# A linear-attention and two-MLP kernel: PSUM shared out anew in the attention, its rounds in nine stretches of like tiling, projections apart from their Vector steps

## The chip, the cores and the metric

The kernel runs on one core of a Trainium2 chip. The metric is the device time of one execution in microseconds (us). Before the change three timed runs gave a median of 804.03 us (803.39 to 804.15).

## What is computed

```python
def phi(x):                                   # x: 4 batches, 8 heads, 576 tokens, 64
    proj = einsum('bhsd,df->bhsf', x, w_phi)  # 128 features
    proj = proj - max(abs(proj), axis=-1)
    return concatenate([exp(proj), exp(-proj)], axis=-1)
q_p, k_p = phi(q), phi(k)
kv  = einsum('bhsf,bhsd->bhfd', k_p, v)
z   = sum(k_p, axis=2)
num = einsum('bhsf,bhfd->bhsd', q_p, kv)
den = einsum('bhsf,bhf->bhs', q_p, z)[..., None] + 1e-06
x = (num / den), heads side by side           # 4 x 576 x 512
h = relu(x @ w_in)                            # 512 -> 1024
conv_out = depthwise convolution of h over 3 tokens with conv_w
x = (h * sigmoid(conv_out)) @ w_out           # 1024 -> 512
u = x + mixing of the tokens through rank 32 (U, V)
out = u + relu(u @ w_ch1) @ w_ch2             # 512 -> 2048 -> 512
```

The activations and q, k, v, w_phi are float32. The other weights are stored as 64-bit numbers and are decoded on the chip into a high and a low part.

## The kernel before

The attention comes first, in eight rounds of four heads each (two pairs of heads; a batch has two rounds). A pair fills the 128 partitions, 64 for each head. The 1152 columns of a round, two pairs of 576 tokens, are cut into three groups of three 128-blocks for either pair. After the attention come the gated layer (`hp` at L610, `x2p` at L662), the mixing of tokens, and the second MLP (`hps` at L859, `po` at L881).

One round i does this, all of it in float32:

- TensorE (PE) projects each of three k groups and three q groups with w (`ppk`, `ppq`, six products of 64x128 each, L289), into a pair of PSUM banks. Vector (DVE) centres the pair into d: a reduction to the largest absolute value (L292) and a subtraction (L294). In the code both are one function, `centred`.
- ScalarE (ACT) makes the k features `ek` from dk (two exponentials, L303 and L304). For q PE first turns the centred group (`tq`, six transposes, L319, into a pair of banks), and ACT makes `et` out of it (two exponentials, L328).
- PE sums `kvp` out of ek and v for either pair (L339) and the sums of ek, `zp` (L353). ACT evicts both (`kt`, `zt`), PE turns them (`pk` L374, `pz` L388), ACT evicts again (`kv` L381, `z` L395).
- PE makes the numerators (`np`, four single banks a round, L407) and the denominators (`dp`, two banks, L432), ACT evicts them as `num` (L418) and `den` (L440).
- The division: four transfers on the queue of SyncE (SP) lay den out over 128 partitions (`dent`, L443), Vector takes the reciprocal (`rec`, in `divide`), one transfer writes it out (`recd`, L451), four read it back spread over 64 partitions each (`rb`, L458), and GpSimd (POOL) multiplies num by rb into `xf` (L462; in the last round Vector does). ScalarE and Vector split xf of the first batch into a high part `xh` (L227) and a low part `xl` (L233) for the gated layer.

Beside this, fourteen pieces of the gated layer's weights (`win`, `wout`, 512 KB each) are decoded, two in a round. A piece is a generator (`split_steps`) that `go_on` moves on by one step: its load on SP (L166) into a raw buffer, of which the pool `stage` has two under that tag; two steps on Vector (L77, L80); a square and the low half on ScalarE (L86, L88); two steps on Vector (L96, L99) and a product on POOL (L100); a cast on ScalarE (L174) and a subtraction and an addition on POOL (L175, L176). L176 is the last to read the raw buffer. `cw_steps` does the same for the small convolution weights, at the very start. The q, k and v of a round are loaded by SP a round ahead, each into one of two buffers.

PSUM has eight banks. In the attention two pools share them:

```python
ps_s = att_ctx.enter_context(tc.tile_pool(name="ps_s", bufs=4, space=PSUM))
ps_p = front_ctx.enter_context(tc.tile_pool(name="ps_p", bufs=2, space=PSUM, side="right"))
```

A tile of `ps_s` is one bank (kvp, zp, np, dp, ...), a tile of `ps_p` a pair (pp, tq). A step that takes a new tile waits until the readers of the tile that had its place are done.

The order is written by hand. `front` is a list of steps, each with a lag: in turn i of the loop a step with lag -1 works for round i-1. On PE, Vector and ScalarE the instructions stand in the order in which this list issues them (`manual_schedule`). On the queues of SP and of POOL the framework's scheduler puts them in order, and there they run one after the other: an instruction that waits holds up all that stand behind it.

Of the kernel before, what the change touches and what calls it, by code (L numbers as in the profile page):

```python
# [18 lines left out]
P = 128  # L19
# [5 lines left out]
def kernel(  # L25
# [103 lines left out]
    def cw_steps():  # L129
        n = 3 * NJ  # L130
        raw = stage.tile([P, 512, 2], I32, tag="raw", name="cw_raw")[:, 0:n, :]
        x = stage.tile([P, 512], I32, tag="x", name="cw_x")[:, 0:n]
        nc.scalar.dma_start(out=raw.rearrange("p n t -> p (n t)"), in_=conv_w.bitcast(I32))
        yield
        widen_head(raw, x)
        yield
        square_and_low(raw)
        yield
        xf, low = widen_rest(raw, x, nc.gpsimd)
        yield  # L140
        nc.vector.tensor_add(cw, xf, low)
        yield
# [126 lines left out]

    def loads_kv(i):  # L270
        for g in range(G):
            load_part("k", k, i, g)
        load_part("q", q, i, 0)
        t = fpool.tile([P, 10, 2, D], F32, tag="v", name=f"v{i}")
        nc.sync.dma_start(out=t.rearrange("p t h d -> p (t h d)"), in_=v[i])
        raw["v", i] = t

    def loads_q(i):
        for g in range(1, G):
            load_part("q", q, i, g)  # L280

    def centred(nm, i, g):
        x = raw.pop((nm, i, g))
        pp = ps_p.tile([P, 2, 512], F32, tag="p", name=f"pp{nm}{i}_{g}")
        for t in range(G):
            c = slice(t * P, (t + 1) * P)
            for s in range(2):
                r = slice(s * D, (s + 1) * D)
                nc.tensor.matmul(pp[:, s, c], lhsT=x[r, c], rhs=w2[r, :], start=True, stop=True)  # L289
        pv = pp[:, :, 0:GC].rearrange("p s (t f) -> p s t f", f=P)  # L290
        m = fpool.tile([P, 2, G, 1], F32, tag="m", name=f"m{nm}{i}_{g}", bufs=4)
        nc.vector.tensor_reduce(out=m[:, :, :, 0], in_=pv, op=ALU.max, axis=AX.X, apply_absolute_value=True)  # L292
        d = fpool.tile([P, 2, G, P], F32, tag="d", name=f"d{nm}{i}_{g}", bufs=3)
        nc.vector.tensor_tensor(out=d, in0=pv, in1=m.to_broadcast([P, 2, G, P]), op=ALU.subtract)  # L294
        return d

    def k_centred(i, g):
        state[i]["dk"].append(centred("k", i, g))

    def k_features(i, g):  # L300
        d = state[i]["dk"][g].rearrange("p s t f -> p (s t) f")
# [3 lines left out]
        state[i]["es"].append(e)  # L305

    def k_tile(i, s, t):
        return state[i]["es"][t // G][:, s * G + t % G, :, :].rearrange("p a f -> p (a f)")

    def q_centred(i, g):  # L310
        state[i]["ds"].append(centred("q", i, g))

    def turn_q(i, g):
        st = state[i]
        d = st["ds"][g]
        ps = ps_p.tile([P, 2, 512], F32, tag="p", name=f"tq{i}_{g}")
# [5 lines left out]
    def q_features(i, g):  # L322
        st = state[i]
        if g == 0:
            st["et"] = apool.tile([P, 2, 2, PT], F32, tag="et", name=f"et{i}", bufs=1)
# [6 lines left out]
    def kv(i, u):  # L332
        st = state[i]
        if u == 0:
            st["kvp"] = ps_s.tile([P, 512], F32, tag="s", name=f"kvp{i}")
# [61 lines left out]
    def numerators(i, u):  # L397
        st = state[i]
        st["np"] = []
        for c in range(2):  # L400
            ps = ps_s.tile([P, 512], F32, tag="s", name=f"np{i}_{u}{c}")
            st["np"].append(ps)
            cs = slice(u * S + c * HC, u * S + (c + 1) * HC)
# [7 lines left out]
    def evict_numerators(i, u):  # L411
# [3 lines left out]
        else:  # L415
            num = apool.tile([P, S], F32, tag="num", name=f"num{i}_{u}", bufs=2)
        for c, ps in enumerate(st.pop("np")):
            nc.scalar.copy(num[:, c * HC : (c + 1) * HC], ps[:, 0:HC])  # L418
# [26 lines left out]
    def divide(i):  # L445
        st = state.pop(i)
        b, g = divmod(i, H // 4)
# [20 lines left out]
    def new(i):  # L468
        state[i] = {"es": [], "ds": [], "dk": [], "tq": {}}

# [9 lines left out]
    def go_on(n):  # L480
        if n in under_way:
            next(under_way[n])

    def step(f, *args):
        return lambda i: f(i, *args)

    def first(i):
        go_on(2 * i - 1)

    def second(i):  # L490
        go_on(2 * i)

# [4 lines left out]
    def first_rests(i):  # L497
        if 4 <= i < 4 + NK:
            split_rest(0, i - 4)

    front = [
        (new, 0),
        (step(k_centred, 0), 0),
        (turn_kv, -1),
        (turned_kv, -1),
        (step(turn_q, 2), -1),
        (step(q_features, 2), -1),
        (turn_sums, -1),
        (turned_sums, -1),
        (first, 0),  # L510
        (first_rests, 0),
        (step(k_features, 0), 0),
        (step(numerators, 0), -1),
        (step(evict_numerators, 0), -1),
        (first, 0),
        (step(k_centred, 1), 0),
        (step(numerators, 1), -1),
        (step(k_features, 1), 0),
        (step(evict_numerators, 1), -1),
        (step(k_centred, 2), 0),  # L520
        (lambda i: begin_piece(2 * i), 0),
        (first, 0),
        (denominators, -1),
        (step(k_features, 2), 0),
        (evict_denominators, -1),
        (first, 0),
        (first_heads, 0),
        (step(q_centred, 0), 0),
        (loads_kv, 1),
        (step(kv, 0), 0),  # L530
        (step(q_centred, 1), 0),
        (loads_q, 1),
        (step(turn_q, 0), 0),
        (step(q_features, 0), 0),
        (divide, -1),
        (second, 0),
        (step(kv, 1), 0),
        (evict_kv, 0),
        (second, 0),
        (step(q_centred, 2), 0),  # L540
        (second, 0),
        (step(turn_q, 1), 0),
        (step(q_features, 1), 0),
        (second, 0),
        (lambda i: begin_piece(2 * i + 1), 0),
        (sums, 0),
        (evict_sums, 0),
    ]

    loads_kv(0)  # L550
    loads_q(0)

    under_way[-1] = cw_steps()
    go_on(-1)
    att_order, rounds_order = ExitStack(), ExitStack()
    att_order.enter_context(tc.manual_schedule(engines={mybir.EngineType.PE}))
    rounds_order.enter_context(tc.manual_schedule(engines={mybir.EngineType.DVE, mybir.EngineType.Activation}))
    for i in range(NU):
        for step, lag in front:
            if 0 <= i + lag < NU:  # L560
                step(i + lag)
    i = NU - 1
    turn_kv(i)
    turned_kv(i)
    turn_q(i, 2)
    q_features(i, 2)
    turn_sums(i)
    turned_sums(i)
# [3 lines left out]
    for u in range(2):  # L572
        numerators(i, u)
        evict_numerators(i, u)
    denominators(i)
    evict_denominators(i)
    rounds_order.close()
# [411 lines left out]
```

## Time and profile before

| | |
|---|---|
| median of three runs | 804.03 us (803.39 to 804.15) |
| the profiled execution | 804.7 us, of which its span, first to last instruction, is 802.9 us |
| mean granted clock of TensorE | 0.997 of full speed |
| TensorE (PE) busy | 792.5 us, 99% of the span |
| Vector (DVE) busy | 521.0 us, 65% |
| ScalarE (ACT) busy | 351.8 us, 44% |
| GpSimd (POOL) busy | 105.5 us, 13% |
| DMA, mean over the span | 72 GB/s |

A row of the timeline gives the start of a group of like instructions in us from the span's start, the time to the end of the last of them, the engine, the line, the operation with its tiles (output <- inputs, numbers left out) and shapes, and xN, the records in the group. Where an engine was idle ahead of a group, a bracket gives that time and what ended it. A matmul's end is modelled, so a PE row can end a little after the next one starts; starts are the better rulers. SPq is SP's queue of DMA issues: its duration is that of the issuing and says nothing of when the data lands.

### The profile page before, as it was taken

What the parts mean: (1) busy time and instruction counts of PE and PEld (TensorE: products, weight loads), DVE (VectorE), ACT (ScalarE), POOL (GpSimd) and SP (SyncE); (2) the same over time, 40 slices, a digit from 0 to 9 for tenths busy, and PEclk for the clock granted to TensorE, in tenths of its full rate; (3) what the DMA queues carried; (4) which work ended last, traced back from release to release, by engine and by line L of the source; (5) the groups of instructions that cost most, each with busy time, mean ns of one, the idle gap of its engine ahead of it and who ended that gap; (6) DMA issues with size and microseconds to landing.
All of it is one profiled execution on the core that took longest, in us unless ns stands there. A gap on an engine that the chain in (4) does not pass through costs nothing.

```text
span 802.9 us, 12634 instructions
## 1 busy us (share of the span) xinstructions
PE 792.5 (99%) x5082; PEld 640.0 (80%) x5082; DVE 521.0 (65%) x825; ACT 351.8 (44%) x625; POOL 105.5 (13%) x112
## 2 busy tenths in 40 slices
PE   8999999999999999999999999999999999999997
PEld 6666666669998888988778788888888888888886
DVE  5777888856989978975368734883496285332322
ACT  4777877776677754654314312341242132111010
POOL 0354445430201220210000000000000000000000
PEclk9999999999999999999999999999999999999999
DMA  7355455412221120112221101220120020000212
GB/s 234 106 176 175 144 156 173 133 32 84 52 69 53 31 96 1 55 52 79 91 78 55 53 0 53 78 81 1 53 77 29 0 80 27 0 1 1 91 66 79
DMA packets 34650, 58.12 MB, mean 72 GB/s; under 512 B 7008, under 2 KB 21472, under 8 KB 34592
## 3 DMA queue, kind: packets, MB, share of 16 engines
q1 hardware_dynamic: 34304, 57.23, 22.4%
q8 instruction: 40, 0.66, 0.3%
q14 instruction: 18, 0.15, 0.1%
q10 hardware_dynamic: 288, 0.09, 0.0%
HBM read 48.77 MB, written 8.46 MB: 71 GB/s over the span
## 4 chain that ended last, share of the span: by engine, by line
PE 82%; DVE 10%; DMA 4%; ACT 2%; issue 1%; SPq 0%; POOL 0%; DVEq 0%; ACTq 0%; POOLq 0%
PE hps L859 23%; PE po L881 23%; PE hp L610 7%; PE x2p L662 7%; PE kvp L339 4%; PE np L407 3%; PE ppk L289 3%; PE ppq L289 2%; PE zp L353 2%; DVE cv L622 2%; PE tq L319 2%; PE dp L432 2%; PE x2m L680 1%; DVE g L630 1%; PE utp L818 1%
## 5 line engine op out<-in xcount | busy, mean ns | idle before, releaser
L865 ACT ACTIVATE hh<-hps 128x512 fp32r<-128x512 f32 (+1 forms) x80 | 44.3, 553 | 223.5 <-PE hps L859 218.9
L866 DVE SCALAR_TENSOR_TENSOR hl<-hps,hh 128x512 fp32r<-128x512 f32 (+1 forms) x80 | 50.8, 635 | 101.6 <-ACT hh L865 101.6
L610 PE MATMUL hp<-xh,win 128*128 128x288 f32 x512 | 105.0, 296 | 0.0
L662 PE MATMUL x2p<-wout,g 128*128 128x512 f32 x384 | 96.1, 392 | 0.5 <-ACT g L629 0.5
L859 PE MATMUL hps<-uh,c1h 128*128 128x512 f32 (+1 forms) x240 | 88.9, 371 | 0.7 <-ACT x L642 0.7
L859 PE MATMUL hps<-ul,c1h 128*128 128x512 f32 (+1 forms) x240 | 88.4, 368 | 0.0
L859 PE MATMUL hps<-uh,c1l 128*128 128x512 f32 (+1 forms) x240 | 88.3, 368 | 0.0
L610 PEld LDWEIGHTS hp<-xh,win 128*128 128x128 f32 x512 | 83.7, 188 | 4.5 <-issue 2.1
L886 DVE TENSOR_TENSOR u<-u,po 128x512 f32<-128x512 f32 x90 | 58.5, 682 | 41.0 <-PE po L881 41.0
L881 PE MATMUL po<-c2h,hh 128*128 128x512 f32 x216 | 84.3, 390 | 0.0
L881 PE MATMUL po<-c2l,hh 128*128 128x512 f32 x216 | 84.2, 390 | 0.0
L881 PE MATMUL po<-c2h,hl 128*128 128x512 f32 x216 | 82.0, 389 | 0.0
L662 PEld LDWEIGHTS x2p<-wout,g 128*128 128x128 f32 x384 | 69.7, 188 | 14.0 <-ACT g L629 0.9
L610 PE MATMUL hp<-xl,win 128*128 128x288 f32 x256 | 75.6, 295 | 0.0
L622 DVE SCALAR_TENSOR_TENSOR cv<-h,cw,cv 128x576 f32<-128x576 f32 x64 | 51.5, 812 | 6.6 <-ACT cv L620 6.2
L859 PEld LDWEIGHTS hps<-uh,c1h 128*128 128x128 f32 x240 | 45.2, 188 | 9.5 <-ACT x L642 1.1
L859 PEld LDWEIGHTS hps<-uh,c1l 128*128 128x128 f32 x240 | 45.2, 188 | 7.8
L859 PEld LDWEIGHTS hps<-ul,c1h 128*128 128x128 f32 x240 | 45.2, 188 | 7.9
L610 PEld LDWEIGHTS hp<-xl,win 128*128 128x128 f32 x256 | 48.2, 188 | 1.7 <-issue 0.8
L655 POOL CAST ghold<-g 128x128 fp32r<-128x128 f32 x32 | 27.2, 854 | 168.9 <-DVE g L630 161.8
L881 PEld LDWEIGHTS po<-c2h,hh 128*128 128x128 f32 x216 | 40.6, 188 | 8.6 <-ACT hh L865 0.8
L881 PEld LDWEIGHTS po<-c2h,hl 128*128 128x128 f32 x216 | 40.6, 188 | 8.6
(490 smaller groups left out, 1447.3 us busy)
## 6 DMA issues: line engine op xcount, KB each, us to landing
v<-in_v_dram SPq DMA_DIRECT2D x8, 640.0 KB, 4.8
kr<-in_k_dram SPq DMA_DIRECT2D x24, 192.0 KB, 3.7
qr<-in_q_dram SPq DMA_DIRECT2D x24, 192.0 KB, 3.7
rb<-recd SPq DMA_DIRECT2D x32, 144.0 KB, 3.5
out_dram<-u SPq DMA_DIRECT2D x18, 256.0 KB, 2.1
u<-x2d SPq DMA_DIRECT2D x14, 256.0 KB, 3.9
x2d<-x SPq DMA_DIRECT2D x10, 256.0 KB, 2.2
c_0r<-in_moe_w_ch_dram SPq DMA_DIRECT2D x2, 512.0 KB, 4.3
```

The lines of the kernel that those rows point to most:

```text
L289: nc.tensor.matmul(pp[:, s, c], lhsT=x[r, c], rhs=w2[r, :], start=True, stop=True)
L339: nc.tensor.matmul(o[s * D : (s + 1) * D, :], lhsT=raw["v", i][:, 5 * u + n, s, :], rhs=k_tile(i, s, 4 * u + n), start=(n == 0), stop=(n = ...
L407: nc.tensor.matmul(ps[r, 0:HC], lhsT=st["kv"][:, u, a, r], rhs=st["et"][:, s, a, cs], start=(a == 0), stop=(a == 1))
L610: nc.tensor.matmul(ps[:, 0:HC], lhsT=win[kk][:, wi, j * P : (j + 1) * P], rhs=xs[b][kk][xi][:, cs], start=(i == 0), stop=(i == 3 * NK - 1),)
L622: nc.vector.scalar_tensor_tensor(out=cv, in0=h[:, t : t + S], scalar=cw[:, t * NJ + j : t * NJ + j + 1], in1=cv, op0=ALU.mult, op1=ALU.add,)
L655: nc.gpsimd.tensor_copy(ghold[:, :, j, off : off + LEFT], g.bitcast(F32)[:, :, rest : rest + LEFT])
L662: nc.tensor.matmul(x2p[t], lhsT=g[:, gi, ts_], rhs=w[wi], start=(j == 0 and i == 0), stop=(j == NJ - 1 and i == 2),)
L859: nc.tensor.matmul(ps[:, 0:w], lhsT=ch[j, 0][wi][:, kc], rhs=x[:, kk, :], start=(n == 0), stop=(n == 3 * NK - 1))
L865: nc.scalar.activation(hh, ps[:, 0:w], AF.Relu)
L866: nc.vector.scalar_tensor_tensor(out=hl, in0=ps[:, 0:w], scalar=0.0, in1=hh.bitcast(F32), op0=ALU.max, op1=ALU.subtract)
L881: nc.tensor.matmul(po[i][t], lhsT=x[:, cs], rhs=w, start=(j == js[0] and n == 0), stop=(j == js[-1] and n == 2))
L886: nc.vector.tensor_add(u, u, p)
```

## The change

- **PSUM.** `ps_s` has two single banks and `ps_p` three pairs, for four and two.
- **Projection apart from centring.** `centred` becomes `project` (PE) and `centre` (Vector), two steps that the list may put apart. A projection's buffer is loaded for the next round right behind it (`project_and_load`), v two rounds ahead (`load_v`).
- **The list `front`** is written anew: ppk_0; pk and pz and tq_2; ppk_1 and ppk_2; the four np; ppq_1, ppq_0, ppq_2; the two dp; kvp of both pairs; tq_0 and tq_1; zp. Vector centres the q groups in the order 1, 0, 2, the last of them at the end of the turn.
- **The pieces** begin at other places, two in a turn as before; the two loads stand before the denominators' eviction. The convolution weights move from the start into round 7, and their load from ScalarE's queue to SP's.

Cut to its core:

```diff
-        nc.scalar.dma_start(out=raw.rearrange("p n t -> p (n t)"), in_=conv_w.bitcast(I32))
+        nc.sync.dma_start(out=raw.rearrange("p n t -> p (n t)"), in_=conv_w.bitcast(I32))
...
-    ps_s = att_ctx.enter_context(tc.tile_pool(name="ps_s", bufs=4, space=PSUM))
-    ps_p = front_ctx.enter_context(tc.tile_pool(name="ps_p", bufs=2, space=PSUM, side="right"))
+    ps_s = att_ctx.enter_context(tc.tile_pool(name="ps_s", bufs=2, space=PSUM))
+    ps_p = front_ctx.enter_context(tc.tile_pool(name="ps_p", bufs=3, space=PSUM, side="right"))
...
-    def centred(nm, i, g):
+    def project(i, nm, g):
...
                 nc.tensor.matmul(pp[:, s, c], lhsT=x[r, c], rhs=w2[r, :], start=True, stop=True)
+        state[i]["pp", nm, g] = pp
+
+    def centre(i, nm, g):
+        pp = state[i].pop(("pp", nm, g))
...
+    def project_and_load(i, nm, g):
+        project(i, nm, g)
+        if i + 1 < NU:
+            load_part(nm, {"k": k, "q": q}[nm], i + 1, g)
...
     def first(i):
-        go_on(2 * i - 1)
+        go_on(2 * i - 2)
     def second(i):
-        go_on(2 * i)
+        go_on(2 * i + 1)
+    def begin_first(i):
+        begin_piece(2 * i - 2)
+    def begin_second(i):
+        begin_piece(2 * i + 1)
...
+    front = [
+        (first, 0), (first_heads, -1),
+        (step(turn_q, 0), -1), (step(turn_q, 1), -1), (evict_kv, -1),
+        (step(q_features, 0), -1), (sums, -1), (step(q_features, 1), -1), (evict_sums, -1),
+        (step(project_and_load, "k", 0), 0),
+        (second, -1), (turn_kv, -1), (turn_sums, -1), (turned_kv, -1), (first, 0),
+        (step(centre, "k", 0), 0),
+        (begin_first, 1), (turned_sums, -1), (second, -1),
+        (step(turn_q, 2), -1), (step(q_features, 2), -1),
+        (step(project_and_load, "k", 1), 0), (step(project_and_load, "k", 2), 0),
+        (back[0], -1),
+        (step(centre, "k", 1), 0), (step(centre, "k", 2), 0),
+        (back[1], -1), (back[2], -1), (second, -1),
+        (step(project_and_load, "q", 1), 0), (step(project_and_load, "q", 0), 0),
+        (first_rests, -1), (step(k_features, 0), 0),
+        (step(project_and_load, "q", 2), 0),
+        (back[3], -1), (begin_second, 0),
+        (step(centre, "q", 1), 0),
+        (back[4], -1), (step(k_features, 1), 0),
+        (step(centre, "q", 0), 0),
+        (back[5], -1), (step(k_features, 2), 0),
+        (first, 1), (divide, -1), (second, 0), (first, 1),
+        (step(kv, 0), 0), (step(kv, 1), 0), (load_v, 2),
+        (step(centre, "q", 2), 0),
+    ]
```

Here `back[0]` to `back[5]` are the numerators of pair 0, their eviction, those of pair 1, theirs, the denominators and their eviction. In the last turn the steps of lag -1 are issued once more for the last round, `back` after the pools of the front are closed, as before.

How this moves the instructions is shown at three places. Names of tiles carry a group or bank number and a running number, and line numbers are those of the program that the row is of. The first place is PE in the middle of a round, with the numerators and denominators of the round before; the program before:

```order
L289 MATMUL ppk_1_384<-w_117,kr_1_220 128x128 x6
L407 MATMUL np_10_395<-et_261,kv_348 64x288 x4
L407 MATMUL np_11_400<-et_261,kv_348 64x288 x4
L289 MATMUL ppk_2_411<-w_117,kr_2_222 128x128 x6
L432 MATMUL dp_0_429<-et_261,z_362 32x288 x8
L432 MATMUL dp_1_438<-et_261,z_362 32x288 x8
L289 MATMUL ppq_0_461<-w_117,qr_0_224 128x128 x6
L339 MATMUL kvp_482<-ek_0_366,v_226 64x256 x6
L339 MATMUL kvp_482<-ek_1_405,v_226 64x256 x4
L289 MATMUL ppq_1_493<-w_117,qr_1_250 128x128 x6
L319 MATMUL tq_0_508<-ident,dq_0_470 128x128 x6
```

and the same stretch of the changed one:

```order
L277 MATMUL ppk_1_368<-w_117,kr_1_176 128x128 x6
L277 MATMUL ppk_2_377<-w_117,kr_2_185 128x128 x6
L393 MATMUL np_00_386<-et_294,kv_341 64x288 x4
L393 MATMUL np_01_391<-et_294,kv_341 64x288 x4
L393 MATMUL np_10_407<-et_294,kv_341 64x288 x4
L393 MATMUL np_11_412<-et_294,kv_341 64x288 x4
L277 MATMUL ppq_1_420<-w_117,qr_1_202 128x128 x6
L277 MATMUL ppq_0_429<-w_117,qr_0_211 128x128 x6
L277 MATMUL ppq_2_441<-w_117,qr_2_223 128x128 x6
L418 MATMUL dp_0_460<-et_294,z_354 32x288 x8
L418 MATMUL dp_1_469<-et_294,z_354 32x288 x8
```

Products of one kind that stood apart now stand side by side, and the four np come one behind the other into two single banks, where they had four.

The second place is SP and POOL in the turn in which the weight pieces win30 and win31 are loaded. SP's queue before:

```order
L267 DMA kr_0_1010<-in_k_dram 128x384
L166 DMA win30r<-in_moe_w_in_dram 128x1024
L267 DMA kr_1_1012<-in_k_dram 128x384
L267 DMA kr_2_1014<-in_k_dram 128x384
L267 DMA qr_0_1016<-in_q_dram 128x384
L443 DMA dent_989<-den_986 32x1x18 x4
L267 DMA qr_1_1042<-in_q_dram 128x384
L166 DMA win31r<-in_moe_w_in_dram 128x1024
L451 DMA recd_96<-rec_1056 128x18
L275 DMA v_1290<-in_v_dram 128x1280
L458 DMA rb_0_1060<-recd_96 64x576 x2
```

and in the changed program:

```order
L267 DMA kr_2_920<-in_k_dram 128x384
L166 DMA win30r<-in_moe_w_in_dram 128x1024
L267 DMA qr_1_963<-in_q_dram 128x384
L166 DMA win31r<-in_moe_w_in_dram 128x1024
L267 DMA qr_0_972<-in_q_dram 128x384
L267 DMA qr_2_984<-in_q_dram 128x384
L429 DMA dent_1024<-den_1021 32x1x18 x4
L437 DMA recd_96<-rec_1034 128x18
L481 DMA v_1073<-in_v_dram 128x1280
L444 DMA rb_0_1038<-recd_96 64x576 x2
L444 DMA rb_1_1043<-recd_96 64x576 x2
```

Both loads of a turn stand ahead of dent, where one stood behind it and ahead of recd. POOL's queue for the two pieces of that turn's raw buffers before:

```order
L462 TENSOR_TENSOR xf_0_793<-num_0_647,rb_0_790 128x576
L100 TENSOR_TENSOR win20r<-win20r 128x512
L175 TENSOR_TENSOR win20x<-win20x,win_690 128x512
L462 TENSOR_TENSOR xf_1_798<-num_1_676,rb_1_795 128x576
L176 TENSOR_TENSOR win_690<-win20x,win20r 128x512
L100 TENSOR_TENSOR win21r<-win21r 128x512
L175 TENSOR_TENSOR win21x<-win21x,win_690 128x512
L176 TENSOR_TENSOR win_690<-win21x,win21r 128x512
```

and in the changed program:

```order
L100 TENSOR_TENSOR win20r<-win20r 128x512
L448 TENSOR_TENSOR xf_0_773<-num_0_672,rb_0_770 128x576
L448 TENSOR_TENSOR xf_1_778<-num_1_718,rb_1_775 128x576
L175 TENSOR_TENSOR win20x<-win20x,win_618 128x512
L100 TENSOR_TENSOR win21r<-win21r 128x512
L176 TENSOR_TENSOR win_618<-win20x,win20r 128x512
L175 TENSOR_TENSOR win21x<-win21x,win_618 128x512
L176 TENSOR_TENSOR win_618<-win21x,win21r 128x512
```

The first piece's product moved ahead of the two xf, and both xf stand ahead of both pieces' L176.

The third place is ScalarE at the end of the attention, in the changed program; before, the casts and copies stand in the same order, with the copy z between the second and the third cast:

```order
L314 ACTIVATE et_2157<-tq_2_2202 128x2x384 x2
L227 CAST xh_0_2466<-xf_0_1041 128x576
L227 CAST xh_1_2470<-xf_1_1046 128x576
L227 CAST xh_2_2474<-xf_0_1311 128x576
L227 CAST xh_3_2478<-xf_1_1316 128x576
L404 COPY num_0_2232<-np_00_2222 128x288
L404 COPY num_0_2232<-np_01_2227 128x288
L404 COPY num_1_2245<-np_10_2235 128x288
```

The four casts `xh` of the second batch still stand ahead of the copy that frees the bank of np_00, and np_10 now takes that bank.

## Rows read from the trace of the kernel before

**Rows 1.** The page, busy time of each engine.

```profile
PE 792.5 (99%) x5082; PEld 640.0 (80%) x5082; DVE 521.0 (65%) x825; ACT 351.8 (44%) x625; POOL 105.5 (13%) x112
```

**Rows 2.** Timeline of PE, two attention rounds (start, us, engine line op).

```profile
22.59 0.94 PE L289 MATMUL ppk<-w,kr 64*128 64x128 f32 x12
...
45.41 0.82 PE L319 MATMUL tq<-ident,dq 128*128 128x128 f32 x6
46.06 0.38 PE L388 MATMUL pz<-ident,zt 128*128 128x128 f32 x2
46.37 2.16 PE L407 MATMUL np<-et,kv 128*64 128x288 f32 x16
48.47 0.94 PE L289 MATMUL ppk<-w,kr 64*128 64x128 f32 x12
...
58.42 0.87 PE L319 MATMUL tq<-ident,dq 128*128 128x128 f32 x6
59.22 2.38 PE L339 MATMUL kvp<-ek,v 128*64 128x256 f32 x20
...
65.50 0.94 PE L289 MATMUL ppk<-w,kr 64*128 64x128 f32 x12
```

**Rows 3.** Windows, 10 to 12 us: PE, PEld, DVE, ACT, POOL, clock, DMA, GB/s.

```profile
10.00:12.00 2.00, 2.00 (x16) 1.58 (x17) 1.83 (x4) 1.72 (x3) 0.00 (x0) 0.51 0.99 382
```

**Rows 4.** Timeline of DVE, the start, and the end of a weight step.

```profile
5.63 0.96 DVE L292 TENSOR_REDUCE mk<-ppk 128x6 f32<-128x768 f32 x1 [5.63 <-PE ppk L289]
...
7.50 0.17 DVE L77 TENSOR_SCALAR cw_x<-cw_raw 128x24 int32<-128x24 int32 x1
...
64.45 0.68 DVE L96 SCALAR_TENSOR_TENSOR win20x<-win20r,win20x 128x512 f32<-128x512 f32 x1
65.17 0.43 DVE L99 TENSOR_SCALAR win20r<-win20x 128x512 int32<-128x512 int32 x1
```

**Rows 5.** Timeline of SP's queue, three rounds of the division.

```profile
35.19 3.74 SPq L443 DMA_DIRECT2D dent<-den  x4
...
97.62 0.33 SPq L166 DMA_DIRECT2D wout00r<-in_moe_w_out_dram  x1
...
99.55 2.44 SPq L443 DMA_DIRECT2D dent<-den  x4
...
104.19 0.33 SPq L451 DMA_DIRECT2D recd<-rec  x1
...
107.39 1.13 SPq L458 DMA_DIRECT2D rb<-recd  x2
...
168.65 0.34 SPq L451 DMA_DIRECT2D recd<-rec  x1
170.12 2.40 SPq L458 DMA_DIRECT2D rb<-recd  x4
```

**Rows 6.** Timeline of POOL, one round (the releaser of idle time in brackets).

```profile
111.94 1.73 POOL L462 TENSOR_TENSOR xf<-num,rb 128x576 f32<-128x576 f32 x1 [9.17 <-DMA rb<-recd]
...
115.15 1.27 POOL L175 TENSOR_TENSOR wout00x<-wout00x,wout 128x512 f32<-128x512 f32 x1
116.38 1.43 POOL L462 TENSOR_TENSOR xf<-num,rb 128x576 f32<-128x576 f32 x1
117.76 1.31 POOL L176 TENSOR_TENSOR wout<-wout00x,wout00r 128x512 fp32r<-128x512 f32 x1
120.21 1.04 POOL L100 TENSOR_TENSOR wout01r<-wout01r 128x512 f32<-128x512 f32 x1 [1.15 <-issue]
```

**Rows 7.** Timeline of PE and ACT at the end of the attention.

```profile
174.22 4.10 PE L407 MATMUL np<-et,kv 128*64 128x288 f32 x32
...
180.61 0.53 PE L610 MATMUL hp<-xh,win 128*128 128x288 f32 x2
...
175.51 1.25 ACT L227 CAST xh<-xf 128x576 fp32r<-128x576 f32 x2
...
178.06 1.32 ACT L418 COPY num<-np 128x288 f32<-128x288 f32 x4
```

More of the change, by code (lines that the diff above doesn't have):

```diff
@@ L268, in load_part @@
         raw[nm, i, g] = t
[L270 to L280, printed above, removed]
-    def centred(nm, i, g):
+    def project(i, nm, g):
         x = raw.pop((nm, i, g))
@@ L323, in q_features @@
         st = state[i]
-        if g == 0:
+        if "et" not in st:
             st["et"] = apool.tile([P, 2, 2, PT], F32, tag="et", name=f"et{i}", bufs=1)
@@ L333, in kv @@
         st = state[i]
-        if u == 0:
+        if "kvp" not in st:
             st["kvp"] = ps_s.tile([P, 512], F32, tag="s", name=f"kvp{i}")
@@ L416, in evict_numerators @@
             num = apool.tile([P, S], F32, tag="num", name=f"num{i}_{u}", bufs=2)
-        for c, ps in enumerate(st.pop("np")):
+        for c, ps in enumerate(st.pop(("np", u))):
             nc.scalar.copy(num[:, c * HC : (c + 1) * HC], ps[:, 0:HC])
@@ L466 @@
     pieces += [lambda j=j: wout_piece(j) for j in range(NJ - 2)]
-    def new(i):
-        state[i] = {"es": [], "ds": [], "dk": [], "tq": {}}
+    pieces += [None, cw_steps]
+    for i in range(NU):
+        state[i] = {"es": {}, "tq": {}}
     under_way = {}
@@ L499, in first_rests @@
             split_rest(0, i - 4)
-    front = [
-        (new, 0),
-        (step(k_centred, 0), 0),
+    back = [
+        step(numerators, 0),
+        step(evict_numerators, 0),
+        step(numerators, 1),
+        step(evict_numerators, 1),
+        denominators,
+        evict_denominators,
+    ]
+    front = [
+        (first, 0),
+        (first_heads, -1),
+        (step(turn_q, 0), -1),
+        (step(turn_q, 1), -1),
+        (evict_kv, -1),
+        (step(q_features, 0), -1),
+        (sums, -1),
+        (step(q_features, 1), -1),
+        (evict_sums, -1),
+        (step(project_and_load, "k", 0), 0),
+        (second, -1),
@@ L504 @@
         (turn_kv, -1),
+        (turn_sums, -1),
         (turned_kv, -1),
+        (first, 0),
+        (step(centre, "k", 0), 0),
+        (begin_first, 1),
+        (turned_sums, -1),
+        (second, -1),
         (step(turn_q, 2), -1),
         (step(q_features, 2), -1),
[L508 to L511, printed above, removed]
-        (step(k_features, 0), 0),
-        (step(numerators, 0), -1),
-        (step(evict_numerators, 0), -1),
-        (first, 0),
@@ L516 @@
-        (step(k_centred, 1), 0),
-        (step(numerators, 1), -1),
-        (step(k_features, 1), 0),
[L519 to L523, printed above, removed]
-        (step(k_features, 2), 0),
[L525 to L531, printed above, removed]
@@ L532 @@
-        (loads_q, 1),
-        (step(turn_q, 0), 0),
-        (step(q_features, 0), 0),
+        (step(project_and_load, "k", 1), 0),
+        (step(project_and_load, "k", 2), 0),
+        (back[0], -1),
+        (step(centre, "k", 1), 0),
+        (step(centre, "k", 2), 0),
+        (back[1], -1),
+        (back[2], -1),
+        (second, -1),
+        (step(project_and_load, "q", 1), 0),
+        (step(project_and_load, "q", 0), 0),
+        (first_rests, -1),
+        (step(k_features, 0), 0),
@@ L535 @@
+        (step(project_and_load, "q", 2), 0),
+        (back[3], -1),
+        (begin_second, 0),
+        (step(centre, "q", 1), 0),
+        (back[4], -1),
+        (step(k_features, 1), 0),
+        (step(centre, "q", 0), 0),
+        (back[5], -1),
+        (step(k_features, 2), 0),
+        (first, 1),
         (divide, -1),
         (second, 0),
+        (first, 1),
+        (step(kv, 0), 0),
         (step(kv, 1), 0),
-        (evict_kv, 0),
-        (second, 0),
-        (step(q_centred, 2), 0),
@@ L541 @@
[L541 to L547, printed above, removed]
-    ]
[L550 to L554, printed above, removed]
+        (load_v, 2),
+        (step(centre, "q", 2), 0),
+    ]
+    for g in (0, 1, 2):
+        load_part("k", k, 0, g)
+    load_part("q", q, 0, 1)
+    load_v(0)
+    for g in (0, 2):
+        load_part("q", q, 0, g)
@@ L555 @@
+    load_v(1)
     att_order, rounds_order = ExitStack(), ExitStack()
@@ L558 @@
     for i in range(NU):
-        for step, lag in front:
+        for f, lag in front:
             if 0 <= i + lag < NU:
-                step(i + lag)
+                f(i + lag)
     i = NU - 1
[L563 to L568, printed above, removed]
+    for f, lag in front:
+        if lag < 0 and f not in back and f is not divide:
+            f(i)
     front_ctx.close()
@@ L571 @@
     ps_h = in_ctx.enter_context(tc.tile_pool(name="ps_h", bufs=3, space=PSUM, side="right"))
[L572 to L576, printed above, removed]
+    for f, lag in front:
+        if f in back:
+            f(i)
     rounds_order.close()
```

22 lines of the change are left out of this document (11 added, 11 removed).

## The prediction, made before the changed kernel ran

> **What bounds the kernel now.** I read the page first: TensorE (PE) is busy 99% of the span [rows 1], so only time that PE spends otherwise can be won. Next the timeline of PE through the attention rounds. A round runs from one ppk of group 0 to the next; two rounds lie between 22.59 and 65.50 [rows 2], so 21.45 us each, and PE has no idle time in them. After the attention the first product of the gated layer, hp, starts at 180.61 [rows 7]. Its order behind that point is the same in both programs, and PE is the bound there, so I take it that whatever hp's start gains or loses, the end gains or loses too. The whole question is when hp starts.
>
> **Price of a change of tiling.** Six transposes of 128x128 take 0.80 us until the next start when kv products of 128x64 follow (58.42 to 59.22), and 0.65 when pz, of their own tiling, follows (45.41 to 46.06) [rows 2]. So 0.15 is paid where the tiling changes. The np products say the same: a half takes 2.10 alone (46.37 to 48.47), two halves in one stretch 4.10 less the 0.07 by which a row's modelled end overlaps the next start, 4.03 [rows 2, 7]: 0.17 less than twice 2.10. The order of before has fifteen stretches a round, that of the change nine: six joins (ppk_1 with ppk_2, three ppq in one, both kv, both np, tq_0 with tq_1). At 0.16 each PE's own round falls from 21.45 to 20.49. The two ends for a join that no row shows (two pp groups side by side) are 0 and 0.3; little hangs on it, as will be seen. The Trainium skill, "TensorEngine Tiling", says in Key Properties that a changed tiling mode drains TensorE, and under Instruction Overhead that each matmul carries some 60 cycles; by the second alone a join saves nothing, since no matmul goes. The third rival has that.
>
> **The start.** Vector centres its first k group from 5.63 to 7.50, so 1.87 a group [rows 4]. In the changed order the third of six projections in the queue behind the first three (ppq_2) needs the PSUM pair that k group 2 leaves: 5.63 + 3 x 1.87 = 11.24, and PE ends ppq_2 at 12.1. Then both kv halves (2.38 each less overlap and one join: 4.45 [rows 2]), two tq (1.45), zp (2.3, taken like a kv half of the same 256 columns): 20.3. But between 10 and 12 us the granted clock was 0.51, half of its upper level of 2.4 GHz, after PE had waited for Vector [rows 3]; PE waits there now too. Ends: 0 and a little over 1 us lost; I take 0.65, nearer to the row. Round 1 starts at 20.95 instead of 22.59. The small cw steps leave this stretch; they were 0.2 us each and hide behind PE's work wherever they go.
>
> **Round 1.** ppk_0 0.87, twelve transposes 1.5, ppk_1 and ppk_2 1.57, np 4.03, three ppq 2.27, dp 2.1: 12.3, and 0.7 until ScalarE has evicted den. The first dent transfer starts at 33.95, where it was 35.19 [rows 5].
>
> **The ring that takes PE's place.** Of the rounds, a second chain must be followed, which goes through SP and POOL. The denominators go den, dent (DMA), rec (Vector), recd (DMA), rb (DMA), xf (POOL). Before the change a weight piece's load waits on SP for one POOL step (L176, a piece's last, which frees its raw buffer), and the dent transfers stand behind that load. In the change two loads stand ahead of dent, and POOL's queue reads xf, xf, L175, L100, L176, L175, L176 before the second may go: POOL must end both pieces of a round first. So each turn holds:
> - SP from that load to dent: it took 1.93 for a load and three more issues [rows 5]; now two follow it, three quarters: 1.45.
> - dent to recd: 99.55 to 104.19, 4.64 [rows 5]. I keep it: three loads were in flight ahead of it, now two, but another weight piece precedes them.
> - recd to rb: 3.20 (104.19 to 107.39), where a weight piece had been issued just ahead of recd, but 1.47 (168.65 to 170.12) where none had [rows 5]. In the change none stands between dent and recd, so 1.47; the other end is 3.20.
> - rb to xf: 107.39 to 111.94, 4.55 [rows 5, 6].
> - POOL: xf 1.7 (as long as the first xf of [rows 6] takes), xf 1.38, L175 1.23, L100 1.0, L176 1.3, L175 1.23, L176 1.3 [rows 6]: 9.15.
>
> Together 21.26. That is above PE's 20.49 and just under the old 21.45: the ring becomes the bound, and of the 0.96 a round that the joins save 0.2 is left. Behind the waiting load on SP stand two q loads and dent; behind rec on Vector stand a weight step, the centring of q group 2 and then of k group 0, and PE's next ppk_0 and ppk_2 wait for the pairs those free. np_10 also waits for np_00's single bank, whose eviction waits for xf to have read the old num. So a late ring does reach PE. The Trainium skill, "DMA: Bandwidth & Descriptors", Anatomy of one DMA, gives a transfer a fixed cost of about 2.0 us; for recd to rb that would make a turn 0.53 longer and the sum below about 0.1 slower than before, an estimate from that page. The row, 1.47, is the same queue and transfer.
>
> **The sum.** A second load that waits so stands ahead of the second to the sixth dent: five turns, 33.95 + 5 x 21.26 = 140.25. From there Vector: reciprocal done at +4.6, a weight step 1.1 (64.45 to 65.60 [rows 4]), q group 2 1.87, a weight step 1.1, k group 0 1.87: +10.55; ppk_2 0.87, np_00 and np_01 2.05: np_10 at 153.7. The other way, over xf, is ready at 0.6 less. Then np_10 and np_11 2.0, ppq 2.27, dp 2.1, kv 4.45, tq 1.45, zp 2.3, twelve transposes 1.5: 169.8. Here the two single banks cost: np_10 of the last round needs num's eviction, which on ScalarE stands behind the last et (1.5) and four xh casts (175.51 to 178.06 less a z copy, 2.3 [rows 7]) and takes 0.45: 174.05, where PE would have been ready at 171.9. Before, four banks let all np products pass [rows 7]. Then 2.0 and 2.1: hp at 178.15, against 180.61: 2.5 us earlier.
>
> The profiled execution took 804.7 for a span of 802.9, 0.7 over the median of the runs, 804.03; the same 2.5 off the median is **801.5 us**, 0.3% faster. No change means within 0.2%, 1.6 us, about what a measurement of this kernel can tell.
>
> **Rivals.**
> - **The ring turns slower, and the kernel is slower.** If recd lands as late as behind a weight piece in before (3.20), a turn is 22.99 and five cost 8.65 more: hp at 186.8, 810.2 us. For it: two pieces of 512 KB now leave within 3 us ahead of dent, and the 3.20 of [rows 5] came with one such piece just ahead. Against: here they leave some 6 us before recd. It decides from a turn of 21.76 on; at 22.1 the loss is 1.7 us. Chance of a turn above 22.08: 0.25.
> - **PE stays the bound.** If POOL and the transfers go round in 20.5 or less, each of seven rounds saves 0.96, the start 1.65, and the last wait takes back what it does: hp at 174.3, 797.7 us. For it: L176 of the second piece need not always stand behind a slow xf. It needs nearly every term at its lower end: 0.15.
> - **The joins save nothing**, so that the change does not do what its nine stretches suggest: a round stays at 21.45, the ring is hidden, only the start's 1.65 and the last wait's 2 remain: hp at 181.0, 804.4 us. [Rows 2] speak against it twice. 0.1.
>
> **How the numbers follow.** My own case, a turn between 20.6 and 21.75, has 0.5; its range alone is 798 to 804. The range that should hold 8 in 10 runs from the second rival with a little better start, 797, to half-way into the first, 807 (a turn of 22.35). Faster by over 0.2%: 0.38 of my own case, the second rival's 0.15 and 0.02 of the third's: 0.55. Same: 0.12 of my own and 0.08 of the third's: 0.20. Slower: the first rival's 0.25.
>
> **What would show it.** A PE timeline with nine stretches, ppk_1 and ppk_2 as one of about 1.6 us and np as one of about 4.0, proves the joins; round 1 starting near 21 the start. Rounds 1 and 2 near 20.5 and from then on near 21.2, with PE idle before ppk_0 or np_10, proves the ring; dent following a weight load by about 1.45 on SP proves where it closes. An idle of 2 us before the last np_10, released by ScalarE, proves the end. I am wrong if the rounds stay at 20.5 to the end, if dent starts as soon as den is evicted, or if recd takes over 2 us to land.

## The result, and the profile after

The changed kernel takes 811.37 us (median of 4 runs, 809.68 to 813.73); the kernel before 804.09 beside it. The ratio is 1.0085, 95% interval 1.0068 to 1.0102: slower by 0.9%, where 801.5 was forecast and 807.0 was the end of the range. The profiled execution of the change took 813.73 us, 9.0 more than that of before. The four executions of the change went with the clock that TensorE was granted: 809.68 and 810.00 us at a mean of 1.000 and 0.999, 812.74 and 813.73 us at 0.998 and 0.997.

I cut the spans where the prediction did: up to the first ppk of round 1, from there to hp, and the rest. Before: 22.59, 158.02, 622.29. After: 21.96, 165.55, 624.39. So the start gave 0.6, the rounds lost 7.5, and the part behind the attention, where I had expected nothing, lost 2.1.

The page's busy line shows that PE does less and waits more; it answers to [rows 1]:

```profile
PE 788.3 (97%) x5082; PEld 639.4 (79%) x5082; DVE 517.2 (64%) x825; ACT 352.0 (43%) x625; POOL 112.8 (14%) x112
```

The timeline of PE in the change: joined stretches of round 1, one later round and the end of the attention (it answers to [rows 2, 7]; in brackets the idle time ahead of a group and what ended it):

```profile
21.96 0.94 PE L277 MATMUL ppk<-w,kr 64*128 64x128 f32 x12
...
24.29 1.65 PE L277 MATMUL ppk<-w,kr 64*128 64x128 f32 x24
25.86 4.10 PE L393 MATMUL np<-et,kv 128*64 128x288 f32 x32
29.90 1.61 PE L277 MATMUL ppq<-w,qr 64*128 64x128 f32 x24
...
42.90 0.94 PE L277 MATMUL ppk<-w,kr 64*128 64x128 f32 x12
...
63.65 0.94 PE L277 MATMUL ppk<-w,kr 64*128 64x128 f32 x12
...
66.62 0.87 PE L305 MATMUL tq<-ident,dq 128*128 128x128 f32 x6 [1.24 <-DVE dq L286]
67.43 0.94 PE L277 MATMUL ppk<-w,kr 64*128 64x128 f32 x12
69.59 0.94 PE L277 MATMUL ppk<-w,kr 64*128 64x128 f32 x12 [1.22 <-issue]
...
87.51 0.94 PE L277 MATMUL ppk<-w,kr 64*128 64x128 f32 x12
...
183.35 2.16 PE L393 MATMUL np<-et,kv 128*64 128x288 f32 x16 [2.08 <-ACT num L404]
...
187.51 0.53 PE L623 MATMUL hp<-xh,win 128*128 128x288 f32 x2
```

Joined, ppk_1 and ppk_2 take 1.57 and the np 4.04 to the next start, as forecast. The first two rounds take 20.94 and 20.75 us. The third takes 23.86: PE waits for the centred q group 2 ahead of tq_2, and again ahead of ppk_2, which the view puts down to issue; ppk_2 starts 0.1 behind the end of the centring of k group 0 (68.53 and 0.96, in Vector's rows below), whose pair of banks it takes. One turn of SP's queue (it answers to [rows 5]):

```profile
57.27 2.45 SPq L429 DMA_DIRECT2D dent<-den  x4
63.66 0.33 SPq L437 DMA_DIRECT2D recd<-rec  x1
64.49 0.34 SPq L481 DMA_DIRECT2D v<-in_v_dram  x1
65.10 3.05 SPq L444 DMA_DIRECT2D rb<-recd  x4
...
79.94 0.33 SPq L166 DMA_DIRECT2D win31r<-in_moe_w_in_dram  x1
80.36 0.86 SPq L267 DMA_DIRECT2D qr<-in_q_dram  x2
81.31 2.44 SPq L429 DMA_DIRECT2D dent<-den  x4
```

POOL in the same turn, from the two xf to the last step of the second piece ([rows 6] before):

```profile
71.02 2.77 POOL L448 TENSOR_TENSOR xf<-num,rb 128x576 f32<-128x576 f32 x2 [2.21 <-DMA rb<-recd]
...
78.61 1.30 POOL L176 TENSOR_TENSOR win<-win21x,win21r 128x512 fp32r<-128x512 f32 x1
```

Vector and ScalarE in the same turn: the reciprocal, what stands behind it, and den:

```profile
63.16 0.18 DVE L435 TENSOR_SCALAR rec<-dent 128x18 f32<-128x18 f32 x1 [4.83 <-DMA dent<-den]
...
65.61 0.96 DVE L286 TENSOR_TENSOR dq<-ppq,mq 128x768 f32<-128x768 f32 x1
...
68.53 0.96 DVE L286 TENSOR_TENSOR dk<-ppk,mk 128x768 f32<-128x768 f32 x1
...
79.42 0.40 ACT L426 COPY den<-dp 128x288 f32<-128x288 f32 x1 [0.53 <-PE dp L418]
```

Two loops run through dent here. One is the forecast's ring: dent, recd, rb, xf, the pieces on POOL, the load of win31, dent: 24.04. The other goes from dent to the reciprocal (5.89), over q group 2 and k group 0 on Vector (until 69.49), ppk_2, np, ppq and dp on PE, until den is evicted (79.82): 22.55. SP then holds dent for another 1.5, and for 1.1 to 2.4 in all five turns; POOL has no gap longer than 0.35 in its steps, and the load of win31 follows the last of them by 0.03. Either loop is longer than PE's own round.

### The profile page after: what moved, and what is told of

It is laid out like the page before. It is cut to its first block, busy times and chain, and to the rows that moved or that the text cites. A ratio compares the mean times of both kernels' runs of the same rounds, so it can differ in the third digit from the quotient of the medians.

```text
span 811.9 us, 12600 instructions
## 1 busy us (share of the span) xinstructions
PE 788.3 (97%) x5082; PEld 639.4 (79%) x5082; DVE 517.2 (64%) x825; ACT 352.0 (43%) x625; POOL 112.8 (14%) x112
## 4 chain that ended last, share of the span: by engine, by line
PE 66%; DVE 3%; DMA 2%; ACT 1%; issue 0%; DVEq 0%; ACTq 0%
PE hps L872 23%; PE po L894 23%; PE x2p L675 9%; PE hp L623 8%; PE x2m L693 1%; PE utp L831 1%; PE tp L716 0%; DMA c_6r<-in_moe_w_ch_dram 0%; DMA c_5r<-in_moe_w_ch_dram 0%; DMA c_1r<-in_moe_w_ch_dram 0%; DMA c_0r<-in_moe_w_ch_dram 0%; DVE u L899 0%; DVE hl L879 0%; ACT xh L227 0%; DVE cv L635 0%
## 5 line engine op out<-in xcount | busy, mean ns | idle before, releaser
L668 POOL CAST ghold<-g 128x128 fp32r<-128x128 f32 x32 | 36.8, 1161 | 163.4 <-DVE g L643 158.1
```

What stands on the lines that cost most here:

```text
L668: nc.gpsimd.tensor_copy(ghold[:, :, j, off : off + LEFT], g.bitcast(F32)[:, :, rest : rest + LEFT])
```

## The experiments

All times in us; turn is the mean from the first to the sixth dent, the spans are cut as above, and the ratio is to the kernel before beside each.

| run | turn | start | rounds | rest | median | ratio (95%) |
|---|---|---|---|---|---|---|
| before | 21.50 | 22.59 | 158.02 | 622.29 | | |
| the change | 22.71 | 21.96 | 165.55 | 624.39 | 811.37 | 1.0085 (1.0068 to 1.0102) |
| q2_first | 22.67 | 20.49 | 166.70 | 623.61 | 812.87 | 1.0105 (1.0083 to 1.0127) |
| dent_ahead | 22.95 | 21.57 | 169.92 | 623.21 | 816.22 | 1.0137 (1.0115 to 1.0159) |
| dent_ahead_q2_first | 21.17 | 20.49 | 158.42 | 625.29 | 806.65 | 1.0021 (1.0006 to 1.0035) |
| late_casts | 22.50 | 20.44 | 162.10 | 623.96 | 810.48 | 1.0061 (1.0040 to 1.0082) |
| both_late_casts | 21.11 | 20.49 | 156.21 | 626.10 | 803.03 | 0.9981 (0.9970 to 0.9993) |
| fetch_moved | 21.03 | 20.65 | 155.24 | 622.61 | 800.36 | 0.9956 (0.9942 to 0.9971) |
| second_step_later | 20.65 | 20.80 | 153.33 | 622.07 | 798.00 | 0.9921 (0.9906 to 0.9936) |
| change_fetch_moved | 23.02 | 22.87 | 168.11 | 622.42 | 811.68 | 1.0096 (1.0068 to 1.0125) |
| dent_ahead_second_later | 21.54 | 20.48 | 159.46 | 625.76 | 807.68 | 1.0047 (1.0030 to 1.0064) |

Some of these spans hold a stretch in which TensorE was granted its lower clock, 1.2 instead of 2.4 GHz: the start of before, of the change and of change_fetch_moved, and the rounds of q2_first (one stretch), dent_ahead (two) and change_fetch_moved (one). Those in the rounds came behind waits of PE of 2.1 to 2.4 us, though not behind every such wait (in the change's profile the np behind the 2.08 took the usual 2.16). Each costs about 1.7 us: in q2_first two np took 3.85 instead of 2.16, and in dent_ahead four took 5.79 instead of 4.10:

```profile
48.61 0.94 PE L277 MATMUL ppk<-w,kr 64*128 64x128 f32 x12 [2.44 <-issue]
49.48 5.79 PE L393 MATMUL np<-et,kv 128*64 128x288 f32 x32
```

**One loop at a time: q2_first.**

```diff
+        (step(centre, "q", 2), 0),
         (first, 1),
         (divide, -1),
...
         (load_v, 2),
-        (step(centre, "q", 2), 0),
```

> Edit: Vector centres q group 2 ahead of the reciprocal instead of behind it; the loads on SP and the ring stay as they are. Theory A (the ring: the second piece's load waits for POOL, and dent waits behind that load) expects the turn from dent to dent to stay at 22.5 to 23 us, since Vector stands idle for 3 to 5 us before the reciprocal and the centring fits into that idle time: hp starts within 2 us of 187.5, time 809 to 812 us. Theory B (the ring is a bystander; what costs is that the reciprocal, which waits for dent to land, stands ahead of the centring on Vector) expects PE's waits before tq_2 (0.7 to 1.2) and ppk_2 (1.2) to go, rounds of 20.8, hp at 178 to 180, time 802 to 804 us.

The turn stayed at 22.67. The waits before tq_2 went, and another took their place: the loop through POOL reaches PE over xf too, since num is copied into a buffer that the last xf must have read. ScalarE and PE in that run:

```profile
70.88 0.70 ACT L404 COPY num<-np 128x288 f32<-128x288 f32 x2 [3.31 <-POOL xf L448]
...
71.33 2.16 PE L393 MATMUL np<-et,kv 128*64 128x288 f32 x16 [1.76 <-ACT num L404]
```

Theory B falls. The time, 812.87, lies just above A's 809 to 812.

**The other loop: dent_ahead.**

```diff
-    ...manual_schedule(engines={mybir.EngineType.DVE, mybir.EngineType.Activation}))
+    ...manual_schedule(engines={mybir.EngineType.DVE, mybir.EngineType.Activation, mybir.EngineType.SP}))
...
-        (begin_second, 0),
...
         (back[5], -1),
+        (begin_second, 0),
```

> Edit: SP's queue takes the order in which the list issues the steps, and the second piece's load is issued behind dent instead of ahead of it (which puts v behind rb as well). Vector's order stays. Theory A expects dent to be issued 0.1 to 0.5 us after den is evicted, turns of 20.8 to 21.3, hp at 177 to 180, time 801 to 804 us, 7 to 10 us less than the change. Theory B expects Vector still to wait 3 us or more for dent to land, PE still to wait 2 us a round before tq_2 and ppk_2, hp at 184 or later, time over 808 us. Theory C (the transfers are slow because weight pieces fill the DMA rings) expects dent to recd to stay over 5 us here, since two pieces a round are still loaded, and rounds of 21.5 to 22.

Theory A falls as I had put it: dent is issued 0.02 behind den's eviction, as A said, and yet the turn is 22.95 and the time 816.22. ScalarE, SP, Vector and PE in one turn of that run:

```profile
82.53 0.40 ACT L426 COPY den<-dp 128x288 f32<-128x288 f32 x1 [0.53 <-PE dp L418]
...
82.95 2.45 SPq L429 DMA_DIRECT2D dent<-den  x4
...
88.09 0.18 DVE L435 TENSOR_SCALAR rec<-dent 128x18 f32<-128x18 f32 x1 [3.85 <-DMA dent<-den]
...
89.27 0.43 DVE L77 TENSOR_SCALAR win31x<-win31r 128x512 int32<-128x512 int32 x1 [0.69 <-DMA win31r<-in_moe_w_in_dram]
...
94.31 0.96 DVE L286 TENSOR_TENSOR dk<-ppk,mk 128x768 f32<-128x768 f32 x1
...
95.37 0.94 PE L277 MATMUL ppk<-w,kr 64*128 64x128 f32 x12 [1.22 <-issue]
```

The loop over Vector and PE is on its own as long as a turn of the change, and the edit made it longer: Vector now also waits for the second piece, whose load lies behind dent (0.69 here, 1.74 the turn before). What theory B expected of this run, hp at 184 or later and over 808 us, came about. Of the 4.4 us by which the rounds are longer than in the change, 3.4 are the two stretches at the lower clock; from the second dent to the sixth the turns are 22.4 on average. Dent to recd took 4.6 to 5.7, though no second piece was ahead of it; theory C had over 5 throughout.

**Both loops: dent_ahead_q2_first**, the two edits together.

> Both edits: dent ahead of the second load, and q group 2 centred ahead of the reciprocal. Theory A expects PE to have no waits left in the rounds: 20.75 each, from 22 to a last zp that ends at 167, hp at 177 with the wait before the last np_10, time 801 us, at most 2 us below the run with dent ahead alone. Theory B expects that this is 5 us or more below the run with dent ahead alone.

hp starts at 178.91 (expected 177) and the turn falls to 21.17. Neither edit gained alone; together they take 7.1 off the rounds' 165.55. So there are two loops, and opening one leaves the other. The time, 806.65, missed theory A's 801 by 5.7, in part because the part behind hp took 625.29; it is 9.6 below dent_ahead, where A had at most 2 and B 5 or more.

**Vector's loop alone: dent_ahead_second_later.** SP's order as in dent_ahead, and Vector's step on the second piece moved away, so that it adds no wait:

```diff
     front = [
         (first, 0),
+        (second, -1),
...
         (divide, -1),
-        (second, 0),
         (first, 1),
```

> Edit: dent ahead of the second load (SP in the list's order), and the second piece's first step behind the first piece's next step on Vector, but q group 2 still centred behind the reciprocal. So the loop through SP and POOL is open, and the one through Vector and PE has its full work and no wait for a late load. By rows of the change that loop is dent to the reciprocal 5.0, reciprocal 0.4, q group 2 1.9, a weight step 1.05, another 1.05, k group 0 1.9, ppk_2 to den evicted 10.3, issue 0.1: 21.7 a turn. Two-loops theory: five turns of 21.6 to 22.3, hp at 182 to 185, time 806 to 809 us. If the loop through SP and POOL was the only one: rounds of 20.75, hp at 177, time 801 us.

The first turns were 21.76, 21.94 and 21.87, as summed; two later ones 20.69 and 21.46, when dent to recd took 4.27 and 4.41 instead of 5.2 to 5.5; PE's rounds were 20.69 and 20.81 then. So in this run the loop is above PE's round while dent lands late. hp, 179.94, came 2 earlier than expected; that the time, 807.68, is in the interval all the same is luck, since the part behind hp took 625.76. Opened without lengthening the other, the loop through SP and POOL alone gives 6.1 of the 7.1 us that both edits together took off the rounds.

**The last wait: late_casts.**

```diff
         if f in back:
             f(i)
+    for kk in range(NK):
+        split_head(1, kk)
```

> Edit: the four casts xh of the second batch are issued behind the last round's num and den copies instead of ahead of them. All theories expect the 2.1 us wait of the last np_10 to go and nothing else: hp at 185.4, time 809.3 us, 0.997 of the change. If the casts then stand in the way of the first h copies, PE waits for a bank after hp and less than 1 us is gained.

The wait is gone (rounds 3.4 shorter, of which the wait is 2.08 and shorter turns 1.1), but the median fell by 0.9 alone, to 810.48; the change's four executions lie 4 us apart, so the trace is the better witness here.

**Together: both_late_casts.**

> Edit: the three edits so far together (dent ahead of the second load in an SP queue that takes the list's order, q group 2 centred ahead of the reciprocal, the second batch's casts behind the last copies). Two-loops theory: the loop through SP and POOL and the loop through Vector and PE are both open, so rounds stay at 20.6 to 21.2 and the 2.1 us wait before the last np_10 goes: hp at 176.5 to 177, time 804 to 805 us, 2 us below the run with the first two. If PE were paced by something else than these waits, hp would stay near 179.

hp is at 176.70, as expected; the time, 803.03, is 1 us below the interval and 3.6 below the run with the first two edits, and it is the first of these that is faster than before. The rest is now 626.10, 3.8 more than before.

**What the rest waits for: fetch_moved.** In the change the load of the mixing weights lands late, and ScalarE, which has the gated layer's h copies queued behind it, waits for it. ScalarE's row in the timeline of the change:

```profile
218.67 0.35 ACT L88 ACTIVATE us_raw<-us_raw 128x160 f32<-128x160 uint32 x1 [3.95 <-DMA us_raw<-in_moe_U_dram]
```

and the DMA view of the change from 213.5 to 218: queues with their packets, MB and share (q8 moves instructions), and an issue with its KB and us to landing:

```profile
q1 hardware_dynamic: 608, 0.15, 15.0%
q8 instruction: 1, 0.02, 1.2%
...
us_raw<-in_moe_U_dram SPq DMA_DIRECT2D x1, 128.0 KB, 4.1
```

The order of the instructions on ScalarE and Vector there is that of before, where the load took 2.3.

```diff
         state[i]["pp", nm, g] = pp
+        if i == 0 and nm == "q" and g < 2:
+            for _ in range(4):
+                nc.tensor.matmul(warm[:, 0:8], lhsT=ident, rhs=ident[:, 0:8], start=True, stop=True)
```

> Edit: as the run with all three, and eight tiny products into the warm-up bank between the first q projections, where PE waits for Vector anyway; they add instructions to PE's program and so move the place in it where a block of instructions is fetched. Theory F: the gated layer loses 2 us because a fetch of PE's instructions falls beside the load of the mixing weights (us_raw), which then lands after 3.4 to 4.1 us instead of 2.3. It expects the load to land after 2.1 to 2.4 again, the first transposed u (utp) 199.3 to 199.8 us behind hp instead of 200.5 to 202, and a time 1.5 to 2.5 us below the run without these products: 802 to 803 us. Theory G (the load is late because the Vector work or the queue ahead of it is late) expects no difference above 0.5 us.

The same view in this run, 201.5 to 205.8, the whole life of that load:

```profile
q1 hardware_dynamic: 608, 0.15, 15.2%
...
us_raw<-in_moe_U_dram SPq DMA_DIRECT2D x1, 128.0 KB, 2.3
```

The transfer on q8 is gone from beside the load, the load lands after 2.3, utp starts 199.55 behind hp instead of 202.85, and the rest falls from 626.10 to 622.61. The median falls by 2.7, a little more than expected. The load is not all of it: in both_late_casts the last round's recd was late too. Its Vector row and its DMA view from 180.5 to 186.5:

```profile
189.21 0.76 DVE L448 TENSOR_TENSOR xf<-num,rb 128x576 f32<-128x576 f32 x1 [1.84 <-DMA rb<-recd]
```

```profile
q8 instruction: 1, 0.02, 1.4%
...
recd<-rec SPq DMA_DIRECT2D x1, 9.0 KB, 3.4
```

That transfer on q8 started 1.1 behind the issue of recd; in fetch_moved it lies 1.1 ahead of it and recd took 1.6. This xf then started 10.8 behind hp instead of 12.5, and the load of the mixing weights was issued 26.2 behind hp instead of 28.4. So the products moved two transfers, and some 2 of the 3.5 us go with the other one.

In all runs of the table: where a transfer on q8 lies 27 to 30 us behind hp (the change and the six runs without the products), the slowest part of the first load takes 3.4 to 4.1 us and the rest 623.2 to 626.1; where it lies 23 to 24 us behind hp (before, and the three runs with the products), 2.2 to 2.3 and at most 622.6. The run psum_as_before below, without the products, agrees: its transfer lies 24.0 behind hp, the load took at most 2.3, and the rest is 622.90. The last recd took 3.3 to 3.4 in three runs, with a transfer on q8 0.8 to 1.1 behind its issue (dent_ahead_q2_first, both_late_casts, dent_ahead_second_later), and these are the three with a rest above 625; where the transfer lies 1.25 or more behind, recd took 1.8 or less.

**The same in the change alone: change_fetch_moved.**

> Edit: the change with the eight tiny products at the start and nothing else. Theory F expects the rounds as in the change (hp at 187 to 188), the load of the mixing weights to land after 2.1 to 2.4 us instead of 4.1, utp 199.3 to 199.8 us behind hp instead of 201.3, and a time 1.5 to 2.3 us below the change's 811.4: 809.1 to 809.9 us. If the fetch has nothing to do with it: 811 to 812 us.

The load landed after 2.1 to 2.2, utp came 199.41 behind hp and the rest was 622.42, as theory F said. The time did not fall (811.68): in the profiled execution, the slowest of four, the start took 0.9 and the turns 0.3 more than in the change's profile, and a stretch at the lower clock lies at the end of the rounds. The two executions at a granted clock of 1.000 took 810.57 and 810.92, where the change's took 809.68. Why the turns were longer stays open; that the load's lateness goes with the transfer is shown, its worth in the change's time is not.

**Vector's last wait: second_step_later**, both_late_casts with the products and with the step moved as in dent_ahead_second_later.

> Edit: as the run before, and Vector decodes the second weight piece's first step behind the first piece's next step instead of right behind the reciprocal, so that the load, which is issued behind dent now, has 1.1 us longer to land. The two-loops theory expects Vector's wait for that load (0.7 to 1.0 a round) to go, and with it PE's last waits before ppk_2 and np_10 (0.2 to 0.7 in some rounds): hp 1 to 1.5 us earlier than in the run before, time 801 to 802 us. If these waits lie beside other waits, nothing moves.

A round of PE in that run:

```profile
42.13 0.94 PE L277 MATMUL ppk<-w,kr 64*128 64x128 f32 x12
...
62.78 0.94 PE L277 MATMUL ppk<-w,kr 64*128 64x128 f32 x12
```

and all its waits between 21 and 176 us (us in total, times, longest):

```profile
PE pz L377 <- ACT zt L355: 0.7, 1, 0.7
PE dp L421 <- ACT num L407: 0.5, 1, 0.5
PE np L396 <- ACT num L407: 0.3, 1, 0.3
```

20.65 a round, 1.5 us of waits in all, hp at 174.13: **798.0 us, 0.8% faster than the kernel before** and 1.6% faster than the change. Expected were 801 to 802; the gain over fetch_moved was larger (2.4 instead of about 1).

**The third pair: psum_as_before.**

```diff
-    ...name="ps_s", bufs=2, ...
+    ...name="ps_s", bufs=4, ...
-    ...name="ps_p", bufs=3, ...
+    ...name="ps_p", bufs=2, ...
```

> Edit: the change with PSUM shared out as before (two pairs, four single banks), orders untouched. If the third pair is what lets the stretches stand together, ppk_1 has to wait for the centring of k group 0 (some 2 us), ppq_2 for that of q group 1 (1.4) and tq_1 for that of q group 2, which stands behind the reciprocal (4 us or more): rounds of 27 to 30, time 840 to 860 us. The wait of the last np_10 goes. If the third pair is worth little, 809 to 815 us.

843.28 us, ratio 1.0484 (1.0462 to 1.0506), rounds of 25.5 to 28.7. PE in one round of that run:

```profile
117.41 0.94 PE L277 MATMUL ppq<-w,qr 64*128 64x128 f32 x12 [1.50 <-issue]
...
128.21 1.09 PE L305 MATMUL tq<-ident,dq 128*128 128x128 f32 x6 [2.52 <-DVE dq L286]
```

A round takes 25.5 at the full clock. The waits were shorter than expected ahead of ppk_1 (0.6 for 2) and tq_1 (at most 3.2 for 4) and longer ahead of ppq_2 (up to 2.3 for 1.4), and the last np_10 does not wait. The three rounds of 27.9 to 28.7 hold a stretch at the lower clock, and the start, 25.36 us, a longer one. That the time fell into the interval is in part luck: with 1.7 us taken off for each of the three it would be 838. The stretches need the third pair; the two single banks it costs are worth one wait of 2 us at the end, and in q2_first, where num waits for xf, six waits of PE before np, 9.1 us in all.

## Why the prediction was wrong

- **The joins** were right. PE's own round was to be 20.49; without waits it is 20.44 to 20.65 in the last version, for 21.45 before. By the Trainium skill, "TensorEngine Tiling", Instruction Overhead, alone a join would have saved nothing; the runs decide against that reading.
- **Start.** 20.95 forecast, 21.96 found. In late_casts, whose program is the same up to there, it was 20.44: there the granted clock was 1.00 from 12 to 14 us, in the change's profile 0.50. I had put this loss at up to a little over 1 us; it was 1.5 in one and none in the other. From round 1 to the first dent, 13.0 forecast, 13.28 found.
- **The step that failed: "Together 21.26".** The ring was the right mechanism, its terms were too small. By the five turns from 35.24 to 148.81: dent to recd 5.33 on average (I kept 4.64), recd to the first xf 6.74 (I had 1.47 + 4.55), the POOL steps with both xf 9.28 (9.15), load to dent 1.37 (1.45): 22.72, where 21.26 was forecast. The four are cut so that each begins where the one before ends, so their sum must come near the 22.71 measured; that they set the pace is seen from SP, which holds dent for the load in every one of the five turns. Five times 1.45 is the larger part of the 9.4 us by which hp missed. The four dent transfers landed 2.1 to 4.6 us after their issue (the median of the four, by turn) where loads stand ahead of them, and 1.7 to 1.9 in the last two rounds, where at most the small load of the convolution weights does. The second term was a mistake in reading [rows 5, 6]: 1.47 came from a turn without a load of v, 4.55 from one in which v was 2.8 us ahead of rb. In the change v lies 0.6 to 1.2 ahead of rb, and the four rb land 4.1 to 5.0 after their issue (the median, by turn); where v stands behind rb (dent_ahead_q2_first), 3.1 to 3.3.
- **The second loop.** I followed the way over Vector once, for the last round, and did not close it. It took 21.8 to 21.9 in the first turns of dent_ahead_second_later, with dent to recd at 5.2 to 5.5, and 22.55 in the turn of the change with 6.39. With the 4.64 that I had kept it would be 20.8 to 21.2, an estimate from these turns: just below the forecast ring and above PE's 20.49. So on the forecast's own terms it would have stayed hidden; it came up with the same term, dent to recd.
- **The last wait** was right: 2.15 forecast, 2.08 found, and it went with the casts.
- **"Whatever hp's start gains or loses, the end gains or loses too"** failed: the same order behind hp took 2.1 longer, 1.9 of it ahead of utp (201.30 behind hp, 199.41 in change_fetch_moved, where the load was in time).
- **The rivals.** The first, slower at 810.2, came nearest, but its reason did not come true: recd to rb took 1.44 to 1.65 in the five turns, near the row I had chosen. (The Trainium skill, "DMA: Bandwidth & Descriptors", Anatomy of one DMA, has about 2.0 for the fixed part of a transfer that GpSimd issues; SP issues these, and the five rows are below it.) It was dent and rb that landed late. Its weight, 0.25, was too small: the forecast turn was 0.5 below the point from which the rival decides, with four transfer times taken from single rows.

## What to carry to other kernels

Joining stretches pays only as far as the loops through the other queues are shorter than the new round: list every loop that comes back to the same transfer, sum each, and open all that are too long, for opening one may gain nothing, or lengthen another. Put a transfer whose result an engine waits for ahead of loads that wait for a buffer, and put behind that wait on the engine only what is not due. Durations of two neighbouring transfers belong together only if they come from the same turn.

## What had not been expected of the hardware

A transfer of instructions beside a load of 128 KB in small parts went with 3.4 to 4.1 us to landing instead of 2.2 to 2.3, and one about 1 us behind the 9 KB of the last recd with 3.3 to 3.4 instead of 1.5 to 2.0. The part behind hp took 622.1 to 622.9 us with neither, 623.2 to 624.4 with the first alone and 625.3 to 626.1 with both. Eight tiny products some 2000 of PE's products earlier moved these transfers. That they are PE's instructions is taken from this move and not shown by the trace.
